# A fixed order list for all engines, a guard in three tasks, the norm's small steps on ScalarE, and 2 KB rows for two loads

## Chip, cores and metric

The kernel runs on one core of a Trainium2 chip. The metric is the device time of one execution in microseconds (us). Three executions of the kernel before took 596.01, 596.94 and 598.41 us; the median is 596.94 us.

## What is computed

Three stages run one after the other on a batch of 4, 768 tokens, 384 channels (8 heads of 48). All is float32; the weights that the program names `moe_` and `moe2_` arrive partly as 8-byte floats.

```python
f = 1 / (1 + exp(-f_logit))
for t in range(S):                                   # gated linear attention
    state = f[:, :, t, :, None] * state + einsum('bhd,bhe->bhde', k[:, :, t], v[:, :, t])
    y[:, :, t] = einsum('bhd,bhde->bhe', q[:, :, t], state)
x = y as (batch, token, channel)
h = gelu_tanh(x @ w_in); u, v = halves of h          # first MLP
v_n = (v - mean) / sqrt(var + 1e-6) * g_ln
x = x + (u * (einsum('ts,bsd->btd', w_sg, v_n) + b_sg)) @ w_out
h = relu(x @ w_in2)                                  # second MLP
out = (h * sigmoid(conv3(h))) @ w_out2
```

## The kernel before, in words

**Attention.** The 24 units (4 batches x 6 chunks of 128 tokens) each load decays, k with q, and v (`ft`, `kin`, `vt`); make running products of the decays by two scans on DVE (L379, L392, tile `pr`) and scale k and q in one DVE multiply (L404, `kin`). TensorE then transposes k (L411), forms state updates (L462), state reads (L492), scores (L425) and the sums over v (L508); DVE makes `mid`, `new` and the masked scores `sm` (L432) between them. ACT copies results into `o`, and SP stores them to the scratch tensor `xd`.

**First MLP.** For each batch, per half of 384 tokens: load `x` from `xd` and split it into a high and a low fp32r part (L655 on ACT, L660 on DVE). Every matrix product is three fp32r products (L649, `mm3`). The items are `v` (128 tokens x 512 columns, 9 matmuls; gelu, then the norm of one row block), `u` (9 matmuls and a gelu), `s` (the token mixing with `wsg`, 18 matmuls; gated on DVE, L992 and L998) and `o` (the product with `w_out`, 12 matmuls, added into `xd` by a DMA of POOL). An `s` of a batch needs the normed parts `vn` of all six `v` of that batch; an `o` needs all of `w_out`; the gate of an `s` needs `cols`, which holds the converted `conv_w` and `g_ln`.

**The norm of one `v`** goes gelu with row sums (ACT, L904), mean (POOL, L907), squares with row sums (ACT, L910), variance plus epsilon and the power -0.5 (POOL, L916 and L917), shift (POOL, L920), norm (ACT, L923), split (ACT L655, DVE L660).

**Weights.** An 8-byte weight piece is loaded as pairs of words (`early` or `stg` tile) and made float32 by one ACT step (L574) and six DVE steps (L575 to L579, L587), then split. `w_in` has 6 such pieces of 128x512, `w_out` 4 of 128x384; the second MLP's weights are converted during the run and spilled to a scratch tensor.

**Second MLP.** For 8 half batches: 8 items of 9 matmuls with relu, three taps, sigmoid, gate and split, then 3 products of 24 matmuls, a copy and a store.

**The order.** Every step is a task added to `Order` with an engine, a supposed duration, and what it must follow. `run` picks tasks one by one by supposed start times and by a rank read from the table `DUE`; the order in which tasks are picked is the order of the instructions on each engine. Each engine then runs its instructions strictly in that order, and waits where an input is not there. TensorE has 3 PSUM banks for the MLP until the attention is done, then 5 more. At that point (`switch`) a guard takes the smallest decay product on DVE, transposes it on TensorE and compares it (L1454 to L1459); `flag` is read at the end, and a general version would run if it were 0.

Of the kernel before, what the change touches and what calls it, by code (L numbers as in the profile page):

```python
# [21 lines left out]
F = 1024  # L22
# [26 lines left out]
HOP = 0.13  # L49

SLACK = 0.2
DMA_RATE, DMA_TIME, TABLE_TIME = 0.21, 1.9, 1.28
# [4 lines left out]
class Hold:  # L57


    def __init__(self):  # L60
        self.left, self.end = 0, 0.0


class Task:
    __slots__ = ("eng", "us", "fn", "after", "rank", "take", "uses", "hold", "table", "kb", "end", "wait", "nexts", "n", "got")


class Order:
# [3 lines left out]


    def __init__(self, rings):
        self.rings = {}
        self.free = dict.fromkeys(("PE", "DVE", "ACT", "POOL", "SP"), 0.0)
        self.dma = 0.0
        self.table = "sigmoid"
        self.ready = {e: [] for e in self.free}
        self.left = 0  # L80
        self.count = 0
        for n, size in rings.items():
            self.ring(n, size)
# [4 lines left out]
    def add(self, eng, us, fn, after=(), rank=0.0, take=(), uses=(), table=None, kb=0.0):  # L88
        t = Task()
        t.eng, t.us, t.fn, t.rank, t.take, t.table, t.kb = eng, us, fn, rank, tuple(take), table, kb  # L90
        t.after = [a for a in after if a is not None]
        t.hold = {n: Hold() for n in t.take}
        t.got = None
# [3 lines left out]
        t.end, t.nexts = None, []  # L97
        t.wait = 0
        for a in t.after:
            if a.end is None:  # L100
                a.nexts.append(t)
                t.wait += 1
        t.n = self.count
        self.count += 1
        self.left += 1
        if not t.wait:
            self.ready[eng].append(t)
        return t

    def start(self, t):  # L110
        at = self.free[t.eng]
        for a in t.after:
            e = a.end + (HOP if a.eng != t.eng or a.kb else 0.0)
            if e > at:
                at = e
        for n in t.take:
            e, _ = self.soonest(n)
            if e is None:
                return None
            if e > at:  # L120
                at = e
        if t.table and t.table != self.table:
            at += TABLE_TIME
        return at

    def soonest(self, name):

        best = None, None
        for n in BANKS if name == "bank" else (name,):
            if n not in self.rings:  # L130
                continue
            slots, i = self.rings[n]
            h = slots[i % len(slots)]
            if h is None:
                return 0.0, n
            if not h.left and (best[0] is None or h.end + HOP < best[0]):
                best = h.end + HOP, n
        return best

    def run(self):  # L140
        while self.left:
            best = None
            for eng, tasks in self.ready.items():
                can = [(at, t) for at, t in ((self.start(t), t) for t in tasks) if at is not None]
                if not can:
                    continue
                soon = min(c[0] for c in can) + SLACK
                at, t = min((c for c in can if c[0] <= soon), key=lambda c: (c[1].rank, c[0], c[1].n))
                if best is None or (at, t.rank) < (best[0], best[1].rank):
                    best = at, t  # L150
            assert best is not None
            self.write(*best)

    def write(self, at, t):
        self.ready[t.eng].remove(t)
        for n in t.take:
            got = self.soonest(n)[1]
            if n == "bank":
                t.got = got
            ring = self.rings[got]  # L160
            ring[0][ring[1] % len(ring[0])] = t.hold[n]
            ring[1] += 1
        t.fn()
        if t.table:
            self.table = t.table
        t.end = at + t.us
        self.free[t.eng] = t.end
        if t.kb:
            self.dma = max(self.dma, at) + t.kb / DMA_RATE / 1000.0
            t.end = self.dma + DMA_TIME  # L170
        for h in t.uses:
            h.left -= 1
            h.end = max(h.end, t.end)
        for x in t.nexts:
            x.wait -= 1
            if not x.wait:
                self.ready[x.eng].append(x)
        self.left -= 1

DUE = {
    "unit load": [
        -548.7, -477.3, -161.3, -153.1, 189.4, 212.0, 364.9, 430.2, 591.1, 816.0, 698.7, 736.9,
        909.1, 1157.3, 1295.0, 1375.7, 1376.1, 1739.4, 1653.8, 1761.4, 3751.4, 2011.8, 2225.9, 3838.8,
    ],
    "unit front": [  # L190
        1385.3, 859.0, 1060.5, -250.2, 1511.2, 1703.3, 1812.9, 2025.9, 2365.2, 229.0, 604.9, 1897.4,
# [1333 lines left out]
```

## Time and profile before

| | |
|---|---|
| device time, three runs | 596.01, 596.94, 598.41 us |
| span of the profiled execution, first to last instruction | 594.3 us |
| busy, share of the span | PE 92%, PE weight load 86%, DVE 74%, ACT 61%, POOL 11% |
| chain that ended last | PE 84%, DVE 8%, POOL 2%, ACT 2%, DMA 2% |
| DMA | 65.94 MB, mean 111 GB/s |

The span is 2.64 us below the median of the three runs; the profile gives no total of its own beyond the span. Matmuls are pipelined and their ends are modelled, so a busy TensorE says that work was in flight. The granted clock column reads 1.00 where nothing throttled; a matmul's duration shows whether the array ran at its lower or its upper clock.

### The profile page before, as it was taken

What the parts mean: (1) busy time and instruction counts of PE and PEld (TensorE: products, weight loads), DVE (VectorE), ACT (ScalarE), POOL (GpSimd) and SP (SyncE); (2) the same over time, 40 slices, a digit from 0 to 9 for tenths busy, and PEclk for the clock granted to TensorE, in tenths of its full rate; (3) what the DMA queues carried; (4) which work ended last, traced back from release to release, by engine and by line L of the source; (5) the groups of instructions that cost most, each with busy time, mean ns of one, the idle gap of its engine ahead of it and who ended that gap; (6) DMA issues with size and microseconds to landing.
All of it is one profiled execution on the core that took longest, in us unless ns stands there. A gap on an engine that the chain in (4) does not pass through costs nothing.

```text
span 594.3 us, 13746 instructions
## 1 busy us (share of the span) xinstructions
PE 546.0 (92%) x5561; PEld 512.2 (86%) x5561; DVE 440.7 (74%) x775; ACT 362.6 (61%) x720; POOL 68.2 (11%) x146
## 2 busy tenths in 40 slices
PE   3553877999999999999999999999999999999995
PEld 2543656998888899889999999999999999999995
DVE  6999898899987986986756344788687685866730
ACT  2534789456788264785347732788777586775830
POOL 2000142000423000433004210110000000000000
PEclk9999997999999999999999999999999999999999
DMA  9877466246858645366334440640210202110011
GB/s 253 203 223 210 111 197 194 59 110 170 201 142 206 187 141 156 99 164 130 107 106 91 131 100 1 152 54 9 81 54 28 69 12 81 46 36 28 14 41 44
DMA packets 55303, 65.94 MB, mean 111 GB/s; under 512 B 26560, under 2 KB 45120, under 8 KB 55232
## 3 DMA queue, kind: packets, MB, share of 16 engines
q1 hardware_dynamic: 51776, 60.27, 35.6%
q0 software_dynamic: 3456, 4.72, 5.8%
q8 instruction: 45, 0.74, 0.5%
q14 instruction: 26, 0.21, 0.1%
HBM read 47.67 MB, written 17.30 MB: 109 GB/s over the span
## 4 chain that ended last, share of the span: by engine, by line
PE 84%; DVE 8%; POOL 2%; ACT 2%; DMA 2%; issue 1%; ACTq 0%; POOLq 0%; DVEq 0%
PE mm L649 45%; PE ma L649 31%; PE at L462 2%; PE at L508 2%; PE at L492 2%; PE at L425 2%; PE pk L411 1%; DMA kin<-in_kq_pairs 1%; DVE kin L404 1%; POOL mv L917 1%; DVE pr L392 1%; DVE pr L379 1%; DVE early L587 1%; DMA bb<-in_moe_b_sg 1%; DVE early L579 1%
## 5 line engine op out<-in xcount | busy, mean ns | idle before, releaser
L1169 DVE SCALAR_TENSOR_TENSOR cv<-h,cols,cv 128x384 f32<-128x384 f32 x128 | 76.2, 617 | 20.7 <-ACT cv L1173 20.2
L649 PE MATMUL mm<-wsg,vn 128*128 128x384 f32 x432 | 81.7, 343 | 0.0
L649 PEld LDWEIGHTS mm<-wsg,vn 128*128 128x128 f32 x432 | 76.1, 191 | 0.9
L649 PE MATMUL ma<-xx,win 128*128 128x386 f32 x378 | 70.3, 338 | 0.0
L649 PEld LDWEIGHTS ma<-xx,win 128*128 128x128 f32 x378 | 66.7, 188 | 0.0
L649 PE MATMUL ma<-wout,gh 128*128 128x384 f32 x224 | 57.4, 337 | 0.0
L649 PE MATMUL mm<-win,x 128*128 128x512 f32 x180 | 48.2, 416 | 0.8 <-ACT x L655 0.8
L649 PE MATMUL mm<-x,win 128*128 128x384 f32 x234 | 46.7, 345 | 1.2 <-ACT win L655 1.0
L660 DVE TENSOR_TENSOR gl<-cv,gh 128x384 fp32r<-128x384 f32 x64 | 35.5, 557 | 16.2 <-ACT gh L655 15.6
L1179 DVE TENSOR_TENSOR cv<-cv,h 128x384 f32<-128x384 f32 x64 | 35.5, 556 | 13.0 <-ACT cv L1176 12.9
L649 PEld LDWEIGHTS mm<-x,win 128*128 128x128 f32 x234 | 40.0, 188 | 2.8 <-ACT win L655 1.4
L1173 ACT ACTIVATE cv<-h,cols 128x384 f32<-128x384 f32 x64 | 39.5, 617 | 3.9 <-DVE gl L660 1.2
L649 PEld LDWEIGHTS mm<-win,x 128*128 128x128 f32 x180 | 33.7, 195 | 8.8 <-ACT x L655 1.1
L649 PE MATMUL mm<-wout,gh 128*128 128x384 f32 x160 | 41.1, 337 | 0.0
L649 PEld LDWEIGHTS ma<-wout,gh 128*128 128x128 f32 x224 | 40.6, 187 | 0.0
L411 PE MATMUL pk<-ident,kin 112*128 112x112 f32 (+1 forms) x96 | 16.2, 299 | 25.0 <-DVE kin L404 24.8
L649 PE MATMUL mm<-xx,win 128*128 128x386 f32 x198 | 38.2, 338 | 0.0
L649 PE MATMUL ma<-wout,gl 128*128 128x384 f32 x112 | 37.7, 337 | 0.0
L649 PE MATMUL mm<-g,wout 128*128 128x384 f32 x192 | 36.6, 340 | 0.0
L655 ACT CAST gh<-cv 128x384 fp32r<-128x384 f32 x64 | 32.4, 506 | 6.2 <-DVE cv L1179 6.1
L649 PEld LDWEIGHTS mm<-xx,win 128*128 128x128 f32 x198 | 35.1, 188 | 0.0
L411 PEld LDWEIGHTS pk<-ident,kin 112*128 112x128 f32 (+1 forms) x96 | 11.4, 153 | 27.2 <-issue 11.9
(120 smaller groups left out, 1127.9 us busy)
## 6 DMA issues: line engine op xcount, KB each, us to landing
kin<-in_kq_pairs SPq DMA_DIRECT2D x24, 448.0 KB, 4.4
stg<-xd SPq DMA_DIRECT2D x16, 576.0 KB, 4.3
ft<-in_f_pairs SPq DMA_DIRECT2D x24, 226.2 KB, 3.3
vt<-in_v_tokens SPq DMA_DIRECT2D x24, 192.0 KB, 4.0
xd<-o SPq DMA_DIRECT2D x96, 48.0 KB, 2.8
stg<-in_moe_w_out SPq DMA_DIRECT2D x12, 384.0 KB, 3.9
xd<-xr POOLq DMA_DIRECT2D x24, 192.0 KB, 4.6
out<-oo SPq DMA_DIRECT2D x24, 192.0 KB, 1.9
```

The source lines that it names most:

```text
L379: self.nc.vector.tensor_tensor_scan(st["pr"][:, 1], st["f"][:, 0:n], self.first, 1.0, op0=ALU.mult, op1=ALU.max)
L411: self.nc.tensor.transpose(pk[:nk, j, 0:R], st["kq"][:, 0, j, 0:nk], self.cst["ident"][0:R, 0:R])
L425: self.nc.tensor.matmul(sc[ts, a, j, :], kt[sl, j, ts], qt[sl, j, ts], start=True, stop=True)
L462: self.nc.tensor.matmul(pu[sl, c, j, :], k2[ts, j, sl], vt[ts, h * D : h * D + D], start=True, stop=True)
L492: self.nc.tensor.matmul(po[g : g + D, c, j, :], state[sl, j, :], st["kq"][sl, 1, j, Q * c : Q * c + Q], start=j == 0, stop=False, skip_gro ...
L508: self.nc.tensor.matmul(po[g : g + D, c, j, :], vt[ts, h * D : h * D + D], sm[ts, a, j, :], start=j == 0 and c == 0 and n == 0, stop=True, ...
L649: self.nc.tensor.matmul(out, l[a], r[b], start=i == 0 and m == 0, stop=i == n - 1 and m == 2)
L655: "ACT", 0.2 + n * 0.0008, lambda: nc.scalar.copy(hi(), src()), after=[after, *wait], rank=rank, uses=uses
L660: lambda: nc.vector.tensor_tensor(lo(), src(), hi(), op=ALU.subtract),
L1169: nc.vector.scalar_tensor_tensor(c, h, self.conv(w, fb), c, op0=ALU.mult, op1=ALU.add)
L1173: nc.scalar.activation(box["c"], box["h"][:, 1 : HALF + 1], AF.Copy, scale=self.conv(1, fb))
L1179: nc.vector.tensor_tensor(box["c"], box["c"], box["h"][:, 1 : HALF + 1], op=ALU.mult)
```

## The change

1. `Order.run` no longer plans. Tasks are issued in the order of a list of 2,037 numbers, `PLACE`; `DUE`, the supposed start times and the rank are out of use. The supposed durations that `add` gets are changed and a lateness per engine is noted, but neither is read when the kernel is built.
2. The guard is three tasks (DVE, TensorE, DVE) that the list places one by one; the opening of the pools for the second MLP is a task without an instruction.
3. In the norm, mean, variance plus epsilon and shift move from POOL to ACT as three activations on 128x1; only the power stays on POOL.
4. `kq_pairs` is laid out with all of k ahead of all of q, so that a partition's row is two runs of 2 KB and not one of 4 KB; `w_in` is laid out in blocks of 256 columns of 8 bytes, so that a piece's row of 4 KB is also two runs of 2 KB.

```diff
-HOP = 0.13
-SLACK = 0.2
-DMA_RATE, DMA_TIME, TABLE_TIME = 0.21, 1.9, 1.28
+LATE = {"PE": 0.31, "DVE": 0.125, "ACT": 0.14, "POOL": 0.06, "SP": 1.95}
...
     def run(self):
-        while self.left:
-            best = None
-            for eng, tasks in self.ready.items():
...
-            self.write(*best)
+        assert sorted(PLACE) == list(range(len(self.tasks)))
+        for count, n in enumerate(PLACE):
+            t = self.tasks[n]
+            assert all(a.done for a in t.after)
+            for name in t.take:
+                got = self.slot(name)
...
+            t.fn()
+            t.done = True
...
+PLACE = [
+    0, 2, 22, 1, 24, 554, 3, 66, 23, 4, 25, 46, 544, 5, 6, 7, 8, 44, 45, 26, 9, 27,
...
-        self.nc.sync.dma_start(st["kq"], self.kq[divmod(u, NCH)])
+        self.nc.sync.dma_start(st["kq"], self.kq[divmod(u, NCH)].rearrange("two r j t -> r two j t"))
...
+W_COLS = 256
+def piece_of(w, r, c, ce):
+    rows, n = slice(r * P, (r + 1) * P), w.shape[2] // 2
+    if w.shape[1] == 1:
+        return w[rows, :, 2 * c : 2 * ce]
+    return w[rows, c // n : ce // n]
...
             nc.scalar.activation(box["v"], box["p"], AF.Gelu_apprx_tanh, accum_out=box["s"][:, 0:1])
-        def mean():
-            nc.gpsimd.tensor_scalar(box["s"][:, 1:2], box["s"][:, 0:1], -1.0 / FH, 0.0, op0=ALU.mult, op1=ALU.add)
+            nc.scalar.activation(box["s"][:, 1:2], box["s"][:, 0:1], AF.Copy, scale=-1.0 / FH)
+        def root():
+            t = box["s"][:, 3:4]
+            nc.gpsimd.tensor_tensor(t, t, self.eps[:, 1:2], op=ALU.pow)
...
+            nc.scalar.activation(box["s"][:, 3:4], box["s"][:, 2:3], AF.Identity, bias=self.eps[:, 0:1], scale=1.0 / FH)
-        def root():
-            t = box["s"][:, 3:4]
-            nc.gpsimd.tensor_scalar(t, box["s"][:, 2:3], 1.0 / FH, LN_EPS, op0=ALU.mult, op1=ALU.add)
-            nc.gpsimd.tensor_tensor(t, t, self.eps[:, 1:2], op=ALU.pow)
-        def off():
-            nc.gpsimd.tensor_tensor(box["s"][:, 1:2], box["s"][:, 1:2], box["s"][:, 3:4], op=ALU.mult)
         def norm():
-            nc.scalar.activation(box["v"], box["v"], AF.Identity, bias=box["s"][:, 1:2], scale=box["s"][:, 3:4])
+            nc.scalar.activation(box["s"][:, 0:1], box["s"][:, 3:4], AF.Copy, scale=box["s"][:, 1:2])
+            nc.scalar.activation(box["v"], box["v"], AF.Identity, bias=box["s"][:, 0:1], scale=box["s"][:, 3:4])
...
-    opened = order.add("DVE", 0.6, switch, after=[t for u in range(N) for t in at.stored[u]])
+    opened = order.add("ACT", 0.0, switch, after=[t for u in range(N) for t in at.stored[u]])
+    t = order.add("DVE", 0.25, reduce, after=at.ended, rank=("open", 0))
+    t = order.add("PE", 0.2, across, after=[t, opened], rank=("open", 0), take=["MA"])
+    order.add("DVE", 0.45, decide, after=[t], rank=("open", 0), uses=[t.hold["MA"]])
...
-    a["kq_pairs"] = _np.stack([by_pairs(k, 0.0), by_pairs(q, 0.0)], axis=3)
+    a["kq_pairs"] = _np.stack([by_pairs(k, 0.0), by_pairs(q, 0.0)], axis=2)
+    w = a["moe_w_in"]
+    a["moe_w_in"] = w.reshape(C, F // W_COLS, W_COLS).transpose(1, 0, 2)
```

**What moves, place 1: SP's first loads.** The names are tile and source; the last number is the tile's. Before, from the program's first load on:

```order
L362 DMA ft0_86<-in_f_pairs 112x517
L366 DMA kin_134<-in_kq_pairs 112x1024
L370 DMA vt_136<-in_v_tokens 128x384
L362 DMA ft1_87<-in_f_pairs 112x517
L366 DMA kin_139<-in_kq_pairs 112x1024
L370 DMA vt_141<-in_v_tokens 128x384
L362 DMA ft2_88<-in_f_pairs 112x517
L366 DMA kin_144<-in_kq_pairs 112x1024
L370 DMA vt_146<-in_v_tokens 128x384
L573 DMA early_149<-in_moe_w_in 128x1024
```

And with the change, from the same place on:

```order
L350 DMA ft0_86<-in_f_pairs 112x517
L358 DMA vt_134<-in_v_tokens 128x384
L350 DMA ft1_87<-in_f_pairs 112x517
L354 DMA kin_137<-in_kq_pairs 112x2x512
L358 DMA vt_139<-in_v_tokens 128x384
L616 DMA early_141<-in_moe_w_in 128x2x512
L350 DMA ft2_88<-in_f_pairs 112x517
L354 DMA kin_145<-in_kq_pairs 112x2x512
L358 DMA vt_150<-in_v_tokens 128x384
L616 DMA early_152<-in_moe_w_in 128x2x512
L350 DMA ft0_86<-in_f_pairs 112x517
```

The first `kin` goes from second to fourth place, the first piece of `w_in` from tenth to sixth, and the second `kin` from fifth to eighth, behind that piece.

**Place 2: DVE around the last `vn` of the first batch**, on which the first `s` waits. Before (`stg_724` is a piece of `w_out`, `vn1_132` the low part of the normed rows, of which the last row here is the sixth):

```order
L579 SCALAR_TENSOR_TENSOR stg_724<-stg_724 128x384
L587 SCALAR_TENSOR_TENSOR stg_724<-stg_724 128x384
L472 TENSOR_TENSOR mid_1240<-at_1220,new_1121 112x192
L478 TENSOR_TENSOR new_1244<-at_1220,mid_1240 112x192
L479 TENSOR_TENSOR new_1244<-new_1244,pend_114 112x192
L660 TENSOR_TENSOR vn1_132<-vg_1088,vn0_131 128x512
L660 TENSOR_TENSOR wsg0_124<-early_1163,wsg0_124 128x768
L432 COPY_PREDICATED sm0_94<-seen_108,at_1268 128x512
L660 TENSOR_TENSOR vn1_132<-vg_1206,vn0_131 128x512
```

With the change (`early_1183` is `conv_w`, 128x24):

```order
L460 TENSOR_TENSOR mid_1177<-at_1141,new_1041 112x192
L466 TENSOR_TENSOR new_1206<-at_1141,mid_1177 112x192
L467 TENSOR_TENSOR new_1206<-new_1206,pend_114 112x192
L703 TENSOR_TENSOR wsg2_126<-early_1158,wsg2_126 128x768
L420 COPY_PREDICATED sm0_94<-seen_108,at_1223 128x512
L703 TENSOR_TENSOR vn1_725<-vg_1112,vn0_724 128x512
L703 TENSOR_TENSOR vn1_725<-vg_1160,vn0_724 128x512
L618 TENSOR_SCALAR early_1183<-early_1183 128x24
L619 TENSOR_SCALAR early_1183<-early_1183 128x24
L367 SCALAR_TENSOR_TENSOR pr_1298<-ft0_86,first_89 112x516
```

From the program's start to the sixth `vn`, DVE's list is the same in kind and number in both but for this: before it holds two conversions of a `w_out` piece (12 steps) and one split of one, and the conversion of `conv_w` (6 steps) with its copy into `cols`; with the change all of these 20 instructions stand behind the sixth `vn`. TensorE's list ahead of the first `s` holds the same 9 units, 6 `v` and 3 `u` in both; with the change the three `u` stand behind the last `v`, before they stand ahead of the fourth.

**Place 3: ACT at the same place.** With the change, from the last two norms of the first batch on (L967, L957 and L970 are the new small steps):

```order
L967 ACTIVATE mv_1161<-mv_1161,eps_116 128x1
L970 ACTIVATE mv_1113<-mv_1113 128x1
L971 ACTIVATE vg_1112<-vg_1112,mv_1113 128x512
L970 ACTIVATE mv_1161<-mv_1161 128x1
L971 ACTIVATE vg_1160<-vg_1160,mv_1161 128x512
L698 CAST vn0_724<-vg_1112 128x512
L698 CAST vn0_724<-vg_1160 128x512
L1007 ACTIVATE u_1254<-mm_1166 128x384
L361 ACT_TABLE_LOAD
L361 ACTIVATE ft0_86<-ft0_86 112x517
L617 ACTIVATE early_1183<-early_1183 128x24
```

Eighteen small steps (three for each of six `v`) now stand on ACT ahead of the last `vn` cast, and the first step of the `conv_w` conversion (L617) stands three instructions behind it, after a table load.

## Rows read from the trace of the kernel before

**Rows 1.** Windows: length; busy us of PE, PEld, DVE, ACT, POOL; clock; DMA; GB/s.

```profile
0.00:20.00 20.00, 8.35 (x176) 7.00 (x180) 14.71 (x21) 7.26 (x15) 3.51 (x18) 1.00 0.93 249
20.00:60.00 40.00, 19.53 (x487) 16.35 (x480) 38.35 (x65) 17.69 (x35) 0.00 (x0) 1.00 0.74 206
60.00:80.00 20.00, 16.92 (x249) 13.31 (x248) 18.23 (x36) 13.52 (x30) 6.87 (x12) 1.00 0.50 146
80.00:100.00 20.00, 13.76 (x303) 10.38 (x304) 17.36 (x31) 18.38 (x38) 5.80 (x13) 0.92 0.68 184
100.00:120.00 20.00, 19.91 (x249) 18.79 (x242) 17.18 (x29) 11.53 (x19) 0.00 (x0) 0.90 0.30 86
120.00:150.00 30.00, 29.78 (x418) 26.55 (x408) 27.76 (x46) 18.90 (x36) 0.53 (x3) 1.00 0.54 149
150.00:300.00 150.00, 149.98 (x2098) 134.67 (x2097) 124.84 (x229) 92.14 (x182) 32.02 (x58) 1.00 0.60 152
300.00:550.00 250.00, 250.00 (x1411) 247.67 (x1410) 165.67 (x293) 164.72 (x331) 19.42 (x44) 1.00 0.25 62
```

**Rows 2.** TensorE's waits from 100 us to the end: total, times, longest.

```profile
PE at L508 <- DVE sm L432: 2.6, 2, 2.4
```

**Rows 3.** TensorE's waits from 0 to 100.8 us, the longest two.

```profile
PE pk L411 <- DVE kin L404: 24.8, 7, 8.6
PE at L508 <- DVE sm L432: 6.2, 5, 2.4
```

**Rows 4.** Timeline of TensorE: first and second `v`, and the first `s`.

```profile
58.83 4.17 PE L649 MATMUL mm<-win,x 128*128 128x512 f32 x9
63.52 2.34 PE L649 MATMUL mm<-win,x 128*128 128x512 f32 x9
...
99.75 1.10 PE L508 MATMUL at<-sm,vt 64*48 64x64 f32 x32 [2.35 <-DVE sm L432]
100.78 7.93 PE L649 MATMUL mm<-wsg,vn 128*128 128x384 f32 x36
```

**Rows 5.** DVE by line and shape: busy us, mean ns of one, idle before.

```profile
L579 DVE SCALAR_TENSOR_TENSOR stg<-stg 128x384 f32<-128x384 uint32 x18 | 10.1, 560 | 0.6
L576 DVE TENSOR_SCALAR stg<-stg 128x384 int32<-128x384 int32 x18 | 6.5, 360 | 0.5
L660 DVE TENSOR_TENSOR wout<-stg,wout 128x384 fp32r<-128x384 f32 x4 | 2.2, 552 | 0.2 <-ACT wout L655 0.2
L577 DVE SCALAR_TENSOR_TENSOR early<-early 128x24 int32<-128x24 int32 x1 | 0.2, 183 | 0.0
```

**Rows 6.** Timeline of DVE: its first instruction, and the sixth `vn`.

```profile
4.41 1.23 DVE L379 TENSOR_TENSOR_SCAN pr<-ft,first 112x516 f32<-112x516 f32 x1 [4.41 <-POOL pend L1443]
...
99.88 0.69 DVE L660 TENSOR_TENSOR vn<-vg,vn 128x512 fp32r<-128x512 f32 x1 [0.18 <-ACT vn L655]
```

**Rows 7.** ACT by line and shape: busy us, mean ns of one, idle before.

```profile
L910 ACT ACTIVATION_READ_ACCUMULATOR junk<-vg,mv 128x1 f32 x24 | 4.5, 188 | 0.0
L574 ACT ACTIVATE stg<-stg 128x384 f32<-128x384 f32 x18 | 10.0, 553 | 2.6 <-DVE stg L577 1.4 <-DMA stg<-in_moe_w_out 1.0 <-DMA stg<-in_moe_w_in 0.2
L655 ACT CAST wout<-stg 128x384 fp32r<-128x384 f32 x4 | 2.0, 510 | 4.3 <-DVE stg L587 4.3
L904 ACT ACT_TABLE_LOAD x4 | 5.1, 1283 | 0.1
```

**Rows 8.** ACT's wait for the norm's last POOL step, 0 to 100.8 us.

```profile
ACT vg L923 <- POOL mv L920: 3.5, 4, 2.3
```

**Rows 9.** DMA issues in 0:20, then in 200:330: KB each, us to landing.

```profile
kin<-in_kq_pairs SPq DMA_DIRECT2D x4, 448.0 KB, 6.9
...
stg<-xd SPq DMA_DIRECT2D x3, 576.0 KB, 4.1
...
stg<-w SPq DMA_DIRECT2D x2, 512.0 KB, 4.6
```

**Rows 10.** The end: the last store's issue on SP.

```profile
588.34 0.33 SPq L1218 DMA_DIRECT2D out<-oo  x1
```

More of the change, by code (lines that the diff above doesn't have):

```diff
@@ L60, in __init__ @@
     def __init__(self):
-        self.left, self.end = 0, 0.0
+        self.left, self.end = 0, 0
 class Task:
-    __slots__ = ("eng", "us", "fn", "after", "rank", "take", "uses", "hold", "table", "kb", "end", "wait", "nexts", "n", "got")
+    __slots__ = (
+        "n", "eng", "us", "cold", "late", "move", "mode", "fn", "after", "rank", "take", "uses", "hold", "table", "got", "done"
+    )
 class Order:
     def __init__(self, rings):
[L75 to L81, printed above, removed]
+        self.rings, self.tasks = {}, []
         for n, size in rings.items():
@@ L154, in write @@
[L154 to L178, printed above, removed]
@@ L253 @@
 SELECTS = set()
+SUMS = set()
 ON_PE = set()
@@ L316, in plan @@
+        lv = add("SP", 0.46, self.load_v, kind="unit load", take=["vt"], kb=192)
         ft, kin, vt = lf.hold["ft"], lk.hold["kin"], lv.hold["vt"]
-        sig = add("ACT", 0.63, self.decays, lf, kind="unit front", uses=[ft], table="sigmoid")
-        fw = add("DVE", 1.23, self.forth, sig, kind="unit front", uses=[ft], take=["pr"])
+        sig = add("ACT", 0.54, self.decays, lf, kind="unit front", uses=[ft], table="sigmoid")
+        fw = add("DVE", 1.14, self.forth, sig, kind="unit front", uses=[ft], take=["pr"])
@@ L327, in plan @@
-        up = add("PE", 0.8, self.update, k2, lv, self.scored, uses=[k2.hold["k2"], vt], take=["A"])
-        a1 = up.hold["A"]
-        mid = add("DVE", 0.36, self.middle, up, before, uses=[a1], take=["mid"])
+        rc = add("DVE", 0.1, self.turn, fw, kind="unit front", uses=[pr], take=["last"])
+        pe = add("ACT", 0.1, self.ends, fw, kind="unit front", uses=[pr])
+        self.ended.append(pe)
+        bw = add("DVE", 1.14, self.back, rc, kind="unit front", uses=[pr, ft, rc.hold["last"]])
@@ L337, in plan @@
+        s5 = add("PE", 0.45, self.states, mid, kq, before, cold=0.8, late=0.28, mode="quarter", uses=[kin, md], take=["A"])
         a2 = s5.hold["A"]
@@ L678, in load @@
             box["steps"][0]()
-        t = S.add("SP", 0.38, load, rank=due("weight load", piece), take=[ring], kb=src.shape[0] * n * 8 / 1000.0, after=after)
+        t = S.add(
+            "SP",
+            0.46,
+            load,
+            rank=due("weight load", piece),
+            take=[ring],
+            kb=src.shape[0] * n * 8 / 1000.0,
+            rate=400.0,
+            after=after,
+        )
         hold = t.hold[ring]
@@ L785, in prep @@
             k = due("weight", 6 + s)
-            t = S.add("SP", 0.38, load, after=[pace[2]], rank=due("weight load", 6 + s), take=["early"], kb=393)
+            t = S.add("SP", 0.46, load, after=[pace[2]], rank=due("weight load", 6 + s), take=["early"], kb=393)
             every = slice(0, S_TOKENS)
@@ L972, in upart @@
         self.all_in.append(m)
-        t = S.add("ACT", 0.51, gelu, after=[m], rank=then, uses=[m.hold["bank"], m.hold["u"]], table="gelu")
+        t = S.add("ACT", 0.38, gelu, after=[m], rank=then, uses=[m.hold["bank"], m.hold["u"]], table="gelu")
         self.t_u[b, hf, db] = t, m.hold["u"]
@@ L1077, in fill @@
             kb = n * cols * P * 4 / 1000.0
-            t = S.add("SP", 0.38, load, after=stored + [opened], rank=due("back load", piece + r // n), take=["stg"], kb=kb)
+            t = S.add("SP", 0.46, load, after=stored + [opened], rank=due("back load", piece + r // n), take=["stg"], kb=kb, rate=212.0 if n == 1 else 400.0)
             hi, lo = ((lambda a=a, r=r: parts()[a][:, r : r + n]) for a in range(2))
```

305 lines of the change are left out of this document (148 added, 157 removed), and 118 rows, old and new, of tables (DUE, PLACE).

## Prediction

> **What bounds the kernel now.** I read the stages of the span first, then TensorE's waits, then the timeline around the place where they end. The stages [rows 1] show two regimes. From 100 us on TensorE is busy for 449.67 of 450 us up to 550 us, and the waits say the same: it waits 2.6 us in all from there to the end, of which 2.4 us is the wait that ends at 99.75 us [rows 2]. So everything behind 100 us is a stream of matmuls of fixed length, which no order makes shorter. Before 100 us TensorE is busy for 58.56 of 100 us, and DVE for 88.65 of them (14.71 + 38.35 + 18.23 + 17.36). What TensorE waits for there is DVE: 24.8 us for the scaled `kin`, 6.2 us for the masked scores [rows 3]. DVE starts at 4.41 us and writes the sixth `vn`, the last input of the first `s`, at 99.88 us [rows 6]; that `s` runs at 100.78 us [rows 4]. DVE's list is therefore the bound up to the first `s`: 88.65 us of work, 4.41 us of start, and some 6.9 us in which it waited. The end adds a fixed tail: the last store is issued at 588.34 us, 6.0 us ahead of the end [rows 10].
>
> The question is thus how much earlier the first `s` starts, and whether TensorE still finds its inputs in time behind it. The sum is made against the span of 594.3 us; the median of the runs lies 2.6 us above it, and I add that at the end.
>
> **The list of orders.** Ahead of the first `s` TensorE does the same units and items as before, so its start moves with DVE's list. What DVE no longer does there is two conversions of a `w_out` piece with one split, and `conv_w`. One conversion is three steps of 0.560 and three of 0.360 us, so two are 5.5 us; the split is 0.55 us; seven small steps at 0.18 us are 1.3 us [rows 5]. That is **-7.4 us**. It could be more, down to -11, if the finer interleaving also saves part of the 6.9 us of waiting.
>
> **The small steps on ScalarE.** Ahead of the sixth `vn` stand 18 new steps; none of this form on one column exists before, and the nearest row, the 128x1 read of the accumulator, takes 0.188 us: 3.4 us [rows 7]. With the `w_out` work go two ACT steps of 0.553 us, one cast of 0.510 us and a small one of 0.2 us: 1.8 us. Net +1.6 us. This counts, because ACT is busy for 18.38 of the 20 us ahead of the first `s` [rows 1] and every norm passes through it. The bounds are 0 (the steps fill waits: ACT waited 3.5 us for the norm's last POOL step [rows 8], which is gone, though the power on POOL and its hop stay) and +3.4. I take **+1.6 us**. POOL loses three steps of each norm; it is busy 5.80 of 20 us there [rows 1], so its own time is worth nothing but that hop.
>
> **The loads in 2 KB rows.** In the first 20 us the DMA engines are busy 0.93 of the time at 249 GB/s [rows 1], and a `kin` takes 6.9 us to land [rows 9]. The list asks more of them: the second `kin` now stands behind a piece of `w_in`, with 2,470 KB up to its end instead of 1,540 KB (the sizes of the issues are 226, 448, 192 and 512 KB). At 249 GB/s that is 9.9 instead of 6.2 us of transfer, and DVE comes to it about 4 us after its first `kin`, so up to 2.5 us of stall could come of it. For faster loads speaks that 576 KB in rows of 1.5 KB land in 4.1 us, while 512 KB in rows of 4 KB take 4.6 us [rows 9]: the longer rows are not the faster ones. With the shorter rows I take **+0.5 us**, between 0 and +2.5, nearer to the `stg` rows than to no gain.
>
> The Trainium skill, page "DMA: Bandwidth & Descriptors", section "Why small descriptors are slow (HBM only)", says the opposite of this edit: each packet carries a fixed overhead of about three cycles, so halving the rows adds overhead. By it the loads would be some 2% slower (an estimate from that page: 3 cycles on 64 beats against 3 on 128), and the term would be at its upper bound. The two rows do not bear it out.
>
> **The clock of TensorE.** The first `v` took 4.17 us and the second 2.34 us for the same nine matmuls: the first ran at the lower of the two levels, 1.2 GHz, after long waits [rows 4]. The same happens at the first `s`: its group of 36 matmuls took 7.93 us, though at the rate of the late stream (250.00 us for 1,411 matmuls, 0.177 us each [rows 1]) it is 6.4 us. Before it stood the 2.35 us wait. With the change three `u` stand between the last `v` and the first `s`, which is 27 matmuls or 4.8 us at that rate, so the wait shrinks. I take **-1.0 us**, between 0 and -1.5.
>
> **What comes back behind the first `s`.** The 7.4 us are not gone. DVE is busy 44.94 of the 50 us from 100 to 150 us [rows 1], so with them 52.3 us would be wanted in 50. And `conv_w` now waits for ACT: its first ACT step stands behind a gelu, a table load of 1.283 us [rows 7] and a sigmoid, so DVE, which has only its last `vn` to do, waits some 2 us right at the first `s`. Queued behind that wait are the next unit's scans and the first gate of an `s`; TensorE can go on for three `s` with its three banks, about 9.5 us. Against it speaks that the list also moves conversions of the second MLP's weights further back, so that DVE's work up to the same place of TensorE stays some 7 us shorter. The bounds are 0 and +4; I take **+2.0 us**, near the 2.3 us by which the stretch would be over-full.
>
> **Edits at nothing.** The guard's three instructions fall where DVE is busy 165.67 of 250 us and TensorE has work queued [rows 1]; without that cover they would cost one small instruction after the other, once. The opening of the pools issues nothing. The changed durations and lateness are not read.
>
> **The sum.** -7.4 + 1.6 + 0.5 - 1.0 + 2.0 = -4.3 us on a span of 594.3: 590.0 us, and with 2.6 us a device time of **592.6 us**, 0.7% faster. About 0.5%, 3.0 us, is what a measurement of this kernel can tell from no change.
>
> **The rivals.**
> *A, the work comes back in full.* DVE is the bound until about 150 us: the over-full 2.3 us, the 2 us for `conv_w` and its other waits in the stretch add up to 6 instead of 2 us. TensorE's stream starts earlier and then stands still. For it: 44.94 of 50 us. Against it: the spills that move back. Then -0.3 us, 596.6 us.
> *B, slower: the loads don't keep up.* DVE runs strictly in its list, and the list wants loads earlier: the first conversion step of `w_in` is DVE's eighth instruction instead of its twentieth, and the next `kin` stands right behind it. If the 2 KB rows bring nothing, DVE stands 2.5 us at each of the first three pieces of `w_in` with the `kin` behind them, 7.5 us and so 7.0 us more than I took; TensorE then waits ahead of the first `s` as before, and the 1.0 us of the clock is not won. That gives 600.6 us. It decides where DVE's idle time ahead of the sixth `vn`, its start apart, grows from 6.9 to over 11 us, since then the -4.3 us are used up. For it: the 0.93 of DMA busy; against it: the two `stg` rows [rows 9].
> *C, more is won.* The list shortens DVE's 6.9 us of waiting by 4 us, or the stream itself from 150 to 300 us, where the weight load is busy only 134.67 of 150 us against 247.67 of 250 later [rows 1]; much of that difference is 512-column matmuls, longer than their load, so I credit 1 us. That gives 592.6 - 5 = 587.6 us. The Trainium skill, page "Perfetto Trace Analysis", section "Identifying the Most-Contended Engine", states that a busy TensorE is no measure of the distance to the best and that the weight load's busy share is; by it up to 15 us would lie open in that stretch.
>
> **How the numbers follow.** The forecast has 0.48, C 0.13, A 0.26, B 0.13. With one or two terms off their middle the forecast reaches from 589 to 595 us. The range goes from C's 587.0 to 598.5 us, which holds A and leaves out B and the far end of C, some 0.2. Faster by over 0.5% is the forecast and C, 0.61; within 0.5% is A and a little of B, 0.27; slower is the rest, 0.12.
>
> **What would show it.** Right: DVE's sixth `vn` ends near 95 us and the first `s` starts at 95 to 97 us, its 36 matmuls take under 7 us, ACT is busy over 90% of the 20 us ahead of it, TensorE waits 1 to 4 us in the 60 us behind it, and the matmuls from there to the end keep their length. The first three DVE waits for a load sum to under 1.5 us. A shows as TensorE's waits for `kin`, `sm` or `mid` behind the first `s` of over 5 us; B as DVE waits for `kin`, `ft` or `early` in the first 40 us. The forecast is wrong if the first `s` is not earlier than 99 us, or if TensorE's waits behind it exceed what was won.

## The result and the profile after

The changed kernel took **603.38 us** (median of four runs, 602.47 to 606.48) against 596.48 us of the kernel before beside it: a ratio of 1.0126, 95% interval 1.0088 to 1.0163. Measured again with six runs it took 602.05 us, 1.0095 (1.0062 to 1.0128). So it is slower by about 1%, some 6 us, and my range of 587.0 to 598.5 us did not hold it. Of all executions one fell into a slower state of the chip, the 604.97 us of the kernel called "joined, loads" below, and its ratio leaves that one out. The profiled execution has a span of 600.7 us, 6.4 us more than before.

The stages of the changed kernel (length; busy us of TensorE, weight load, DVE, ScalarE, POOL; clock; DMA share; GB/s), to be laid beside [rows 1]:

```profile
0.00:20.00 20.00, 4.96 (x88) 4.02 (x88) 10.28 (x15) 5.40 (x11) 3.51 (x18) 1.00 0.88 209
20.00:60.00 40.00, 22.71 (x562) 18.70 (x562) 38.02 (x67) 18.30 (x36) 0.00 (x0) 1.00 0.64 186
60.00:80.00 20.00, 16.56 (x262) 13.37 (x263) 16.06 (x23) 14.93 (x34) 1.45 (x2) 1.00 0.72 203
80.00:100.00 20.00, 16.88 (x293) 12.98 (x295) 14.89 (x26) 19.34 (x47) 2.65 (x4) 1.00 0.61 159
...
150.00:300.00 150.00, 149.22 (x2014) 130.48 (x2013) 113.97 (x210) 99.77 (x214) 20.42 (x22) 1.00 0.58 150
```

DVE did lose work ahead of the first `s`: 79.25 us of it lie in the first 100 us instead of 88.65. But the first `s` is where it was. TensorE's timeline there, with two rows from further on:

```profile
100.62 3.42 PE L692 MATMUL mm<-wsg,vn 128*128 128x384 f32 x18 [0.16 <-ACT u L1007]
104.48 6.57 PE L692 MATMUL mm<-wsg,vn 128*128 128x384 f32 x36 [0.45 <-ACT u L1007]
...
305.36 3.46 PE L692 MATMUL ma<-wsg,vn 128*128 128x384 f32 x18 [1.29 <-ACT o L545]
...
594.49 0.34 PE L692 MATMUL ma<-wout,gl 128*128 128x384 f32 x1
```

The first `s` starts at 100.62 us, before at 100.78 [rows 4]. From there to the end of the last matmul TensorE needs 494.2 us (594.49 + 0.34 - 100.62). Before, the last matmul was this one:

```profile
587.42 0.33 PE L649 MATMUL mm<-wout,gl 128*128 128x384 f32 x1
```

It ended at 587.75 us, so TensorE needed 487.0 us for the same groups. So **nothing was won ahead of the first `s`, and 7.2 us were lost behind it**; the tail behind the last matmul is 0.7 us shorter (5.9 instead of 6.5 us).

**Where DVE's gain went.** DVE's waits up to 101.2 us (engine and line, what it waited for, us in total, times, longest):

```profile
DVE pr L367 <- ACT ft L361: 4.7, 1, 4.7
DVE wsg L703 <- ACT wsg L698: 3.1, 2, 1.6
DVE kin L392 <- DMA kin<-in_kq_pairs: 3.0, 2, 1.8
DVE vn L703 <- ACT vn L698: 1.9, 3, 1.2
DVE new L467 <- ACT pend L375: 1.9, 1, 1.9
DVE pr L367 <- ACT pend L375: 1.6, 1, 1.6
DVE mid L458 <- PE at L450: 1.3, 1, 1.3
DVE mid L460 <- PE at L450: 1.2, 1, 1.2
DVE early L618 <- ACT early L617: 0.3, 1, 0.3
```

They sum to 19.0 us, of which 4.7 us are DVE's start. The same view of the kernel before sums to 8.2 us, of which 4.4 us are the start:

```profile
DVE pr L379 <- POOL pend L1443: 4.4, 1, 4.4
DVE x L660 <- ACT x L655: 1.3, 1, 1.3
DVE mid L472 <- PE at L462: 1.0, 1, 1.0
DVE vn L660 <- ACT vn L655: 1.0, 3, 0.5
DVE sm L432 <- PE at L425: 0.5, 1, 0.5
```

The 10.8 us more of waiting eat the 9.4 us less of work. SP's queue shows where the first of them come from (its issues, in order of time):

```profile
0.82 0.40 SPq L350 DMA_DIRECT2D ft<-in_f_pairs  x1
1.28 0.42 SPq L358 DMA_DIRECT2D vt<-in_v_tokens  x1
1.75 0.42 SPq L350 DMA_DIRECT2D ft<-in_f_pairs  x1
2.21 0.43 SPq L354 DMA_DIRECT2D kin<-in_kq_pairs  x1
2.68 0.46 SPq L358 DMA_DIRECT2D vt<-in_v_tokens  x1
3.19 0.43 SPq L616 DMA_DIRECT2D early<-in_moe_w_in  x1
3.66 0.46 SPq L350 DMA_DIRECT2D ft<-in_f_pairs  x1
...
7.55 0.38 SPq L350 DMA_DIRECT2D ft<-in_f_pairs  x1
```

The first `kin`, without which DVE can't finish its first unit, stands fourth. The third `ft` in the queue (3.66 us) is the fourth unit's; the third unit's is the one at 7.55 us, behind two pieces of `w_in`, and DVE's third scan waits for it by way of ScalarE (1.6 us, put down to `pend`, the copy that stands there on ScalarE).

**Where the 7.2 us behind the first `s` went.** The waits that the profile names there are few (TensorE from 100 us to the end, the same view as [rows 2]):

```profile
PE ma L692 <- ACT o L545: 1.3, 1, 1.3
PE at L532 <- DVE sm L420: 0.9, 2, 0.5
PE mm L692 <- ACT u L1007: 0.6, 2, 0.4
PE mm L692 <- DVE x L703: 0.2, 1, 0.2
```

That is 3.0 us. The rest hides in TensorE's busy time, which is 149.22 of 150 us from 150 to 300 us and says nothing. The weight load does: it fell from 134.67 us for 2,097 loads [rows 1] to 130.48 us for 2,013, so less was done in that stretch. TensorE's timeline shows why, in two `u` groups of the same nine matmuls (start, duration; the pair with an asterisk is the part of the array that is used, rows by columns):

```profile
110.89 1.74 PE L692 MATMUL mm<-x,win 128*128 128x384 f32 x9
112.46 0.55 PE L399 MATMUL pk<-ident,kin 112*128 112x112 f32 x4
...
230.45 0.65 PE L516 MATMUL at<-kin,mid 48*48 48x64 f32 x16
231.03 1.83 PE L692 MATMUL mm<-x,win 128*128 128x384 f32 x9
232.79 0.69 PE L413 MATMUL at<-kin 48*64 48x64 f32 x32
```

Between full-width groups the nine matmuls take 1.57 us from start to start (110.89 to 112.46); between two attention groups that use a quarter of the array they take 1.76 us (231.03 to 232.79). Each stay in the attention between full-width groups costs about **0.2 us**. The kernel before issues a unit's state reads and scores one behind the other; counted in the order of instructions, TensorE goes 45 times from a quarter-array group to a full-width one behind the first `s` (the transpositions of k, on 112 rows, are counted with the full-width ones). The new list puts something between them in 15 units, 14 of them behind the first `s`: 59 times. Fourteen more at 0.2 us are 2.8 us. The Trainium skill, page "TensorEngine Tiling (Array Packing)", section "Key Properties", states that a change of tiling mode drains TensorE; it gives no duration. That such a stay costs 0.2 us here agrees with it.

### The profile page after: what moved, and what is told of

Its sections match the earlier page's. It is cut to its first block, busy times and chain, and to the rows that moved or that the text cites. A ratio compares the mean times of both kernels' runs of the same rounds, so it can differ in the third digit from the quotient of the medians.

```text
span 600.7 us, 13677 instructions
## 1 busy us (share of the span) xinstructions
PE 553.2 (92%) x5561; PEld 514.0 (86%) x5561; DVE 432.3 (72%) x775; ACT 375.9 (63%) x794; POOL 45.2 (8%) x74
## 5 line engine op out<-in xcount | busy, mean ns | idle before, releaser
L692 PEld LDWEIGHTS ma<-xx,win 128*128 128x128 f32 x396 | 70.2, 189 | 0.1
L692 PE MATMUL mm<-wout,gh 128*128 128x384 f32 x192 | 49.3, 337 | 0.0
L692 PE MATMUL ma<-wout,gh 128*128 128x384 f32 x192 | 49.2, 337 | 0.0
L1224 ACT ACTIVATE cv<-cv 128x384 f32<-128x384 f32 x64 | 32.7, 522 | 22.1 <-DVE cv L1217 21.9
L703 DVE TENSOR_TENSOR gl<-cv,gh 128x384 fp32r<-128x384 f32 x64 | 34.6, 554 | 11.7 <-ACT gh L698 10.6
L961 POOL TENSOR_TENSOR mv<-mv,eps 128x1 f32<-128x1 f32 x24 | 20.5, 852 | 287.8 <-ACT mv L967 250.5
L545 ACT COPY o<-at 48x512 f32<-48x512 f32 x48 | 27.9, 581 | 17.8 <-PE at L532 14.4
L692 PEld LDWEIGHTS mm<-x,win 128*128 128x128 f32 x216 | 36.8, 188 | 1.9 <-DVE win L703 0.4
L692 PEld LDWEIGHTS mm<-wout,gh 128*128 128x128 f32 x192 | 34.9, 188 | 0.0
L692 PEld LDWEIGHTS ma<-wout,gh 128*128 128x128 f32 x192 | 34.9, 188 | 0.0
L367 DVE TENSOR_TENSOR_SCAN pr<-ft,first 112x516 f32<-112x516 f32 x24 | 29.5, 1228 | 7.1 <-ACT ft L361 4.7
```

The lines of the kernel that those rows point to most:

```text
L367: self.nc.vector.tensor_tensor_scan(st["pr"][:, 1], st["f"][:, 0:n], self.first, 1.0, op0=ALU.mult, op1=ALU.max)
L545: self.nc.scalar.copy(st["out"][sl], st["o"][sl])
L692: self.nc.tensor.matmul(out, l[a], r[b], start=i == 0 and m == 0, stop=i == n - 1 and m == 2)
L703: lambda: nc.vector.tensor_tensor(lo(), src(), hi(), op=ALU.subtract),
L961: nc.gpsimd.tensor_tensor(t, t, self.eps[:, 1:2], op=ALU.pow)
L1224: nc.scalar.activation(box["c"], box["c"], AF.Sigmoid)
```

## The experiments

I had two theories: **the start** (loads and ScalarE make DVE wait, and the list inherits it) and **the middle** (the list loses on TensorE behind the first `s`); rivals were the 2 KB rows and the norm's small steps on ScalarE. The changed kernel itself was measured a second time:

> The changed kernel unaltered, measured beside the next run so that its ratio rests on more than four executions: 602.4 to 604.4 us, ratio to the kernel before 1.010 to 1.015, first s at 100 to 102.5 us.

It came out just below this on all three counts (602.05 us, 1.0095, 99.65 us).

The table holds all runs; the paragraphs refer to it. "First `s`" is its start in the profiled execution, one for each kernel, "stream" the time from there to the end of the last matmul.

| kernel | us, median (runs) | ratio to before, 95% | first `s` | stream |
|---|---|---|---|---|
| before | 596.48 (4) | 1 | 100.78 | 487.0 |
| after | 603.38 (4) | 1.0126, 1.0088 to 1.0163 | 100.62 | 494.2 |
| after, again | 602.05 (6) | 1.0095, 1.0062 to 1.0128 | 99.65 | 494.3 |
| order of before | 596.58 (12) | 1.0004, 0.9991 to 1.0018 | 100.43 | 488.6 |
| 4 KB rows | 604.01 (6) | 1.0138, 1.0112 to 1.0163 | 102.22 | 493.3 |
| start of before | 610.05 (5) | 1.0245, 1.0222 to 1.0268 | 100.52 | 500.8 |
| start of after | 606.83 (6) | 1.0179, 1.0145 to 1.0214 | 99.83 | 497.2 |
| joined | 600.68 (6) | 1.0079, 1.0050 to 1.0107 | 99.78 | 492.5 |
| loads | 601.67 (6) | 1.0073, 1.0048 to 1.0098 | 99.24 | 494.5 |
| norm on POOL | 601.41 (6) | 1.0074, 1.0051 to 1.0097 | 99.41 | 492.7 |
| joined, norm | 600.65 (6) | 1.0077, 1.0048 to 1.0105 | 99.72 | 492.3 |
| joined, loads | 598.44 (12) | 1.0046, 1.0019 to 1.0073 | 96.38 | 491.1 |
| all three | 597.13 (12) | 1.0017, 1.0002 to 1.0032 | 96.73 | 490.6 |
| all three, `pend` early | 598.57 (12) | 1.0047, 1.0024 to 1.0071 | 98.04 | 490.3 |
| all three, four waits moved | 606.86 (6) | 1.0167, 1.0137 to 1.0198 | 98.83 | 499.6 |

### The list, or the other edits

In the first kernel the numbers of `PLACE` are replaced by the order in which the planner of the kernel before picks the same tasks; the guard's three tasks stand where it stood. All other edits stay.

> The changed kernel with one part undone: the tasks are issued in the order in which the kernel before issues them; 2 KB rows, the norm's small steps on ScalarE and the three guard tasks stay. If the loss of 6.9 us is the list's, at its start or behind it, this runs within 2 us of the kernel before (594.5 to 598.5 us). If it comes from the 2 KB rows or from the steps on ScalarE, this is slower than the kernel before by 3 us or more (over 599.5 us), with DVE's sixth vn later than 101 us.

Level with the kernel before. **Without the list there is no loss**: 2 KB rows, steps on ScalarE and guard together cost nothing under the old order. Whether they cost something under the new one is another question. The 2 KB rows were also undone alone under the new list:

```diff
-        self.nc.sync.dma_start(st["kq"], self.kq[divmod(u, NCH)].rearrange("two r j t -> r two j t"))
+        self.nc.sync.dma_start(st["kq"], self.kq[divmod(u, NCH)])
...
-    a["kq_pairs"] = _np.stack([by_pairs(k, 0.0), by_pairs(q, 0.0)], axis=2)
-    w = a["moe_w_in"]
-    a["moe_w_in"] = w.reshape(C, F // W_COLS, W_COLS).transpose(1, 0, 2)
+    a["kq_pairs"] = _np.stack([by_pairs(k, 0.0), by_pairs(q, 0.0)], axis=3)
```

> The changed kernel with k and q and w_in laid out as before, so that these loads are in 4 KB rows again; the list and all else as changed. If the 2 KB rows slow the first loads, this is at least 2 us faster than the changed kernel (601 us or less) and DVE's waits for kin in the first 20 us shrink from 3.0 to under 1.5 us. If the rows are without effect, it is within 1.5 us of the changed kernel (602 to 605 us). If they help, as I had put into the sum, it is slower by 1 us or more.

Within the interval of the changed kernel: the length of the rows shows no effect under the new list, either way. DVE's waits for `kin` sum to 2.8 us here and to 3.0 with 2 KB rows.

### Halves of the two lists

The order of one kernel up to the first `s`, then the tasks that are left in the order of the other. (The two orders begin with other column blocks of the first batch's first half, so two of these change places; up to nine loads and four DVE tasks move a little where a buffer's turn asks for it.)

> The order of the kernel before up to the first s, then the order of the new list, so that the two w_out conversions stand ahead of the first s again and DVE has less to do behind it. Theory middle (the new list loses behind the first s: attention pieces spread singly between the MLP's matmuls, some 0.2 us for each change of kind, and waits for them): about as the changed kernel, 600 to 604 us, with the first s near 101 us. Theory start (the new list's start, its loads and ScalarE, eats what was to be won, and what follows only inherits DVE's backlog): the backlog is gone, so 597 us or less.

> The mirror image: the new list up to the first s, then the order of the kernel before, with the steps that it had ahead of the first s (the w_out conversions, conv_w) coming right behind it. Theory middle: the bad stretch is gone, so 595 to 599 us, unless the w_out conversions that now follow the first s make TensorE wait for them, which would show as waits for g, kin or sm at 101 to 115 us. Theory start: the start is as bad as in the changed kernel and the conversions come on top, 602 us or more.

Both are slower than either parent, and the first is slower than either theory had it, so these two don't tell start from middle: half a list doesn't fit the other half. What TensorE waited for behind the first `s` shows the seam, first with the start of before, then with the start of after:

```profile
PE at L532 <- DVE sm L420: 4.2, 3, 3.0
```

```profile
PE pk L399 <- DVE kin L392: 6.3, 1, 6.3
```

The second is what I had named beforehand: TensorE waits 6.3 us for the next unit's `kin`, to which DVE comes only behind the `w_out` conversions that stand right behind the first `s`. That is a price for bringing the deferred work back in one lump.

### One place at a time

Joined: in 15 units the state reads' number moves to just ahead of the scores' number, as here for one unit (211 and 212):

```diff
-    644, 210, 211, 751, 228, 730, 212, 229,
+    644, 210, 751, 228, 730, 211, 212, 229,
```

Loads: the first numbers of `PLACE`, those of SP (0 to 2 are the first unit's `ft`, `kin`, `vt`; 22 to 24 the second's; 44 to 46 the third's; 66 the fourth's `ft`; 554 and 544 two pieces of `w_in`):

```diff
-    0, 2, 22, 1, 24, 554, 3, 66, 23, 4, 25, 46, 544, 5, 6, 7, 8, 44, 45, 26,
+    0, 1, 2, 22, 23, 24, 44, 554, 45, 46, 544, 3, 4, 25, 5, 6, 7, 8, 66, 26,
```

Norm on POOL: the three steps go back to `nc.gpsimd.tensor_scalar` and `tensor_tensor`, at their places in the list.

> The changed kernel with TensorE's order changed in 15 units: the state reads are moved back to stand right ahead of the scores of the same unit, as they do in the kernel before; nothing else moves. Behind the first s TensorE then goes 45 times from an attention group to a full-width group instead of 59 times. Theory change of kind: a full-width group right behind an attention group takes 0.2 us longer (nine 128x384 matmuls 1.77 instead of 1.57 us), so 14 fewer give 2.7 us: 600 to 601.5 us. Rival waits: the time is lost in waits for sm, o and u alone, and this is within 1 us of the changed kernel (602.4 to 604.4 us).

> The changed kernel with SP's first eleven loads in another order: the first two units' ft, kin and vt, then the third unit's ft, then the pieces of w_in, and the fourth unit's ft (which the new list loads ahead of the third's) last. Theory loads: DVE's waits of 1.13 and 1.85 us for kin and of 1.64 us for the third unit's scan go, so DVE's list and the first s come 3 to 4 us earlier (97 to 98 us) and the run takes 599.5 to 601 us. Rival ScalarE: ScalarE is busy 19.34 of the 20 us ahead of the first s, so what DVE gains at the start it waits for later; the first s moves by less than 1.5 us and the run is within 1.5 us of the changed kernel.

> The changed kernel with the norm's mean, variance plus epsilon and shift on POOL again, each at the place in the list where its ScalarE step stood. Theory ScalarE: 18 small steps of some 0.2 us less ahead of the first s give ScalarE 3.6 us, and as it is full there the first s comes 1.5 to 3 us earlier and the run is 1.5 to 3 us faster than the changed kernel (600.4 to 602 us). Rival: the three more hops of each norm to POOL and back cost as much as the steps did, and the run is within 1.5 us of the changed kernel or slower.

Each is 0.4 to 2.7 us below the two measurements of the changed kernel, and each interval overlaps with the second of those. Alone they settle little, and the first `s` of the last two (99.24 and 99.41 us) misses what their theories had expected; the pairs and the profiled stages do more.

> Both edits at once, the joined state reads and scores and the loads in the other order. If both theories hold the gains add up to 5.5 to 7 us and the kernel before is reached (596.5 to 598 us). If only one holds, the gain is that one's; if the loads only shift the waits, 600 to 601.5 us.

> State reads joined to scores and the norm's small steps on POOL, the loads in the new list's order. With the all-three kernel this tells what the loads' order is worth on top. If the three edits act independently: 603.4 - 2.7 - 2.0 = 598.7 us, and the loads are worth 1.6 us on top of it; if loads and norm feed the same wait ahead of the first s, this is already level with the all-three kernel (597 us).

> The changed kernel with three edits at once: state reads joined to scores, the first loads in the other order, the norm's small steps on POOL. Alone they gave 2.7, 1.7 and 2.0 us, and the first two together 4.9. If the three act in different places (TensorE behind the first s, DVE in the first 20 us, ScalarE in the 20 us ahead of the first s) they add up: 596 to 598 us, level with the kernel before, with the first s at 94 to 97 us. If the loads and the norm both only feed the same wait ahead of the first s, little comes on top of the two: 598 to 600 us.

The three together bring the ratio from 1.0126 and 1.0095 to 1.0017, within 0.3% of the kernel before. The columns of the table say where. *Loads*: the time falls by 3.5 us between joined with norm and all three, whose intervals don't touch (2.2 us between joined and joined with loads, where they do). With the state reads joined the first `s` comes 3.0 to 3.4 us earlier (99.78 to 96.38, 99.72 to 96.73), unjoined by about 1 us only. But the last two kernels of the table with the loads moved, all three and four waits moved, have the same list up to the first `s` and start it at 96.73 and 98.83 us, so a single pair says little. The five with the loads moved start it at 96.38 to 99.24 us, 97.8 on the mean; the six with the changed kernel's order of loads, in 2 KB rows, at 99.41 to 100.62 us, 99.8 on the mean. The order of the loads is worth some 2 us there. In the first 20 us a `kin` lands in 5.9 us instead of the 10.6 us of the changed kernel; first the changed kernel's row, then that of all three (KB each, us to landing):

```profile
kin<-in_kq_pairs SPq DMA_DIRECT2D x3, 448.0 KB, 10.6
```

```profile
kin<-in_kq_pairs SPq DMA_DIRECT2D x3, 448.0 KB, 5.9
```

*Joined*: the stream shrinks by 1.8 us from the changed kernel, 3.4 us beside loads, 0.4 us beside norm. The traces say why these differ. Summed from each matmul's start to the next one's, state reads, scores, transpositions of k and `u` groups together take 3.0, 3.1 and 3.1 us less in these three pairs, near the 2.8 us of the count; but TensorE's idle time behind the first `s` is longer by 2.4, 0.8 and 2.8 us. So the price of the changes is there each time, and other waits take part of the gain back. *Norm*: the first `s` doesn't move (99.78 and 99.72; 96.38 and 96.73), the stream shrinks by 0.2 to 1.6 us, and joined with and without norm are level (joined with loads and all three lie 1.3 us apart, with intervals that overlap). So ScalarE's steps are not shown to cost anything, though they are dearer than I took (0.20, 0.29 and 0.29 us; ScalarE's groups up to 101 us, by line):

```profile
L967 ACT ACTIVATE mv<-mv,eps 128x1 f32<-128x1 f32 x6 | 1.8, 294 | 0.3
L970 ACT ACTIVATE mv<-mv 128x1 f32<-128x1 f32 x6 | 1.7, 290 | 0.0
L957 ACT ACTIVATE mv<-mv 128x1 f32<-128x1 f32 x6 | 1.2, 203 | 0.2
```

Eleven of the 12 executions of joined with loads spread from 595.58 to 603.48 us, wider than those of the kernel before (594.22 to 599.03 beside them).

### Single waits

With the three edits the first `s` starts 4.05 us before that of the kernel before, and the stream is 3.7 us longer; TensorE's named waits in it sum to 3.2 us, before to 0.2 us. Two kernels went after what is left.

> The same three edits, and ScalarE's copy of the ninth unit's chunk-end products (pend), for which DVE waited 1.9 us shortly ahead of the first s, moved up by 14 of ScalarE's tasks. If DVE's waits there still decide, 1 to 2 us less than with the three edits (594.5 to 596.5 us). If ScalarE's own list is the bound there, no change (within 0.7 us), and DVE waits longer for the w_sg or vn casts instead.

Nothing is won: it is 1.4 us above all three, more than the rival allowed, though the intervals overlap. In the waits the rival holds: the one for `pend` is gone, but DVE's waits for ScalarE's casts grew; first all three, then `pend` early:

```profile
DVE vn L703 <- ACT vn L698: 3.6, 3, 1.6
DVE wsg L703 <- ACT wsg L698: 2.7, 2, 1.7
```

```profile
DVE vn L703 <- ACT vn L698: 4.9, 3, 2.8
DVE wsg L703 <- ACT wsg L698: 3.8, 2, 2.9
```

> The three edits, and four single tasks moved at the places where TensorE still waits behind the first s: the first s in a new PSUM bank no longer stands right behind the last attention group (1.29 us of wait for ScalarE's copy of o), a copy of an o product is moved up on ScalarE (0.55 us), and two sums over v stand one item later (0.28 and 0.44 us of wait for sm). If what is still lost behind the first s is these waits of the list, 2 to 2.6 us go: 594.5 to 595.5 us, below the kernel before by 0.2 to 0.4%. If it is DVE's and ScalarE's deferred work that comes back, other waits take their place and this is within 0.7 us of the three edits (596.4 to 597.8 us).

Neither: it is 9.7 us slower than the three edits. Two of the four moves put a unit's sum over v one item later, and so its stores. SP's longest wait for `o` from 150 to 210 us grew from 4.3 to 7.3 us, and what stands behind it in SP's queue was issued later: the load of `x` at 193.69 instead of 189.25 us, and the `ft` that ScalarE waits for below at 195.14 instead of 191.68 us; 2.1 us of each is the later first `s`. That `ft` also took longer, some 7.0 us to ScalarE's use of it instead of 4.4 us. One row of SP's waits, then one each of SP's, ScalarE's, DVE's and TensorE's timeline:

```profile
SPq L552 <- ACT o L545: 17.6, 4, 7.3
```

```profile
195.14 0.43 SPq L350 DMA_DIRECT2D ft<-in_f_pairs  x1
...
202.12 0.64 ACT L361 ACTIVATE ft<-ft 112x517 f32<-112x517 f32 x1 [4.83 <-DMA ft<-in_f_pairs]
...
203.83 1.36 DVE L703 TENSOR_TENSOR x<-stg,x 128x1152 fp32r<-128x1152 f32 x1 [5.04 <-ACT x L698]
...
205.86 4.18 PE L692 MATMUL mm<-win,x 128*128 128x512 f32 x9 [4.18 <-DVE gt L1038]
```

So, as far as these rows tell, waits of 0.3 and 0.4 us on TensorE, taken away by later sums, came back as one of 4.2 us by way of three queues; which of the four moves did it was not tried. The wait cost more than its length: behind it, from 203.8 to 210.7 us, the granted clock reads 0.50, and the nine matmuls at 205.86 us take 4.18 us, nine equal ones at 211.33 us 2.35 us. TensorE's waits for ScalarE's copies of `o` products grew too, from 0.5 to 2.2 us in all. Whether the 3.7 us behind the first `s` are the deferred conversions as such or waits of this list stays open; no version ran that beats the kernel before.

## Why the prediction was wrong, step by step

**"A stream of matmuls of fixed length, which no order makes shorter."** This is the step that failed most. No order that ran made it shorter, but this one made it longer, by 7.2 us (494.2 against 487.0). I had read the busy share and the named waits, and neither holds the price of a change between quarter-array and full-width groups. It could have been read before: there, too, one `u` takes 1.77 us between attention groups (228.48 to 230.25 us) and another 1.57 (234.60 to 236.17 us). Fourteen more changes are 2.8 us (the sum over state reads, scores, transpositions and `u` groups says 3.1 us), the named waits 3.0 us (before, behind the first `s`, 0.2 us), the clock gave back some 1.2 us, and nearly 3 us are spread over `s`, `v` and `o` groups and the second MLP's first products, which I can't assign.

**What comes back behind the first `s`, +2.0 us (0 to +4).** The place was right, but of the 7.2 us above only 1.1 us are named waits for DVE. The wait for `conv_w` that I named is there: 1.7 us of DVE's time behind the last `vn`, waiting for ScalarE's step behind the table load. But it shows in none of TensorE's named waits; and an over-full DVE, rival A's reason, was not it either. From 100 to 150 us DVE is busy 45.9 us, 0.9 more than before, and TensorE's waits for `kin`, `sm` and `mid` sum to 0.9 us, far from A's 5 us.

**The list of orders, -7.4 us.** The work went, even 9.4 us by the first 100 us. The step took DVE's waits of 6.9 us as a constant that could only shrink. By the named waits they grew by 10.8 us. After the loads and the joins are mended and the norm is back on POOL the first `s` does come 2 to 4 us earlier than before (98.83 and 96.73 us in two kernels with the same list up to there), where the first three terms gave -5.3 together.

**Loads, +0.5 us (0 to +2.5).** I asked whether the rows are faster and priced the second `kin`. Rows are without effect, so what I had read from the `stg` rows doesn't hold for these loads. The opposite rule, of the Trainium skill, page "DMA: Bandwidth & Descriptors", section "Why small descriptors are slow (HBM only)", doesn't show either; the estimated loss of 2% on these loads is below what the runs can tell. The order of the issues was what cost: 3.0 us for `kin`, of which 1.1 for the very first one, and 1.6 us for the third unit's scan, whose `ft` stood behind the fourth's. The first was visible in the part of the order that I showed, the second wasn't looked for. By the runs it is worth some 2 us at the first `s`.

**Small steps on ScalarE, +1.6 us.** They cost 4.7 us of ScalarE ahead of the sixth `vn` instead of 3.4 (six norms at 0.79 us), and nothing that shows at the first `s`. The row that I took, an accumulator's read, has no operand of one value per partition; the step without one takes 0.20 us, the two with one 0.29. The Trainium skill, page "ScalarE: Activation LUTs", section "What ACT_TABLE_LOAD costs", states some 93 ns for each such operand, and the trace agrees.

**The clock, -1.0 us.** Right, in size too: two `s` took 7.77 us from start to start before; now three take 10.27 us, 0.45 us of it a wait. That is 3.27 instead of 3.89 us for one, some 1.2 us for the two.

**Guard and opening, 0.** Right under the order of before. Under the new list the opening costs 1.29 us: the first `s` in a new PSUM bank stands right behind the last attention group and waits for ScalarE's copies out of it. I had put the guard's cover down to queued work, and not looked at what the opening is followed by.

**The rivals.** B was the nearest: DVE's idle time ahead of the sixth `vn` passed its 11 us (19.0 us of named waits, 4.7 of them the start), and the first `s` stayed. Its reason was half right: `kin`, yes, but not the pieces of `w_in` (0.3 us), and the waits for ScalarE's `wsg`, `vn` and `pend` took more (6.9 us). Its 600.6 us held 2.0 of the stream's 7.2 us. C's credit of 1 us from 150 to 300 us has the wrong sign; there the weight load's share fell. It was the column of TensorE that showed the loss, and so the rule that I cited there (the Trainium skill, page "Perfetto Trace Analysis", section "Identifying the Most-Contended Engine") is borne out as a way of reading, not as a promise of 15 us.

## What to carry to other kernels

A busy engine is not a fixed length: before calling a stream fixed, compare the same group's time between different neighbours, and count in the new order how often the neighbours change. When a list moves work off an in-order engine, read the whole queue that feeds it (here SP's first ten issues) against the order in which the engine will ask; the saved work turns into waits one for one where the feed doesn't move along. And change such a list in a few places at once only with a measurement for each: four moves against waits of 0.3 to 1.3 us cost 9.7 us.

## What I had not expected of the hardware

Two sets of nine equal matmuls took 1.57 and 1.76 us, by their neighbours alone. The granted clock of TensorE from 20 to 60 us read 1.00 in the kernel before [rows 1] and 0.50 under its order with the other edits, while a transposition of k took the same 0.98 us in both; here are the rows, first that of the kernel before:

```profile
26.21 0.98 PE L411 MATMUL pk<-ident,kin 112*128 112x112 f32 x4 [2.84 <-DVE kin L404]
```

```profile
20.00:60.00 40.00, 18.87 (x448) 15.65 (x440) 38.82 (x66) 17.88 (x35) 0.00 (x0) 0.50 0.72 203
...
25.66 0.98 PE L399 MATMUL pk<-ident,kin 112*128 112x112 f32 x4 [2.85 <-DVE kin L392]
```

The same four transpositions take 0.55 us at 112.46 us, so in that stretch the array ran at the lower of its two levels (1.2 and 2.4 GHz) in both, whatever the column says. The trace of the kernel before holds no record of the clock ahead of 62.9 us, and the column reads 1.00 there; so a 1.00 doesn't always mean that nothing throttled. And the same order of loads gave DVE 10.28, 11.63 and 11.72 us of work in the first 20 us in three profiled executions (the third with 4 KB rows), with the first `s` at 100.62, 99.65 and 102.22 us: the landing of the first loads varies by more than some of the effects that were looked for.
